# One buffer per chunk for the later quarters' gated values, chunk sums behind the hh sum, and the split of the last pairs in two parts

## The chip, the cores and the metric

The kernel runs on one core of a Trainium2 chip. The metric is the device time of one execution in microseconds (us); lower is better. All times below are in us unless a unit stands beside them. The engines are TensorE (PE in the profile; its weight loads are PEld), VectorE (DVE), ScalarE (ACT), GpSimd (POOL) and SyncE (SP), whose queue issues the DMA transfers.

## The reference

One layer in two halves, on x of 2048 rows and 448 columns, in float32:

```python
h  = x + Re(DFT_seq(DFT_hid(layernorm(x))))
n  = layernorm(h)
h2 = h + (gelu(n @ w_gate) * (n @ w_up)) @ w_down      # 448 -> 1792 -> 448
```

The transforms are products with given cosine and sine matrices. The kernel computes each float32 product from float16 parts: a value is split into a high half (its float16) and a low half (what is left, as float16), and high x high, high x low and low x high are added up.

## The kernel before

**The stages.** Up to about 460 us the kernel does the two Fourier products (lines 481 to 606). What the change touches comes after them: the gate and up products, the gating and the down product, a loop of 42 steps `t`. The 2048 rows are four quarters. Steps 0 to 13 take quarters 0 and 1 together (512 columns at a time), steps 14 to 27 quarter 2, steps 28 to 41 quarter 3 (256 columns). In each of the three passes a step handles one of the 14 blocks of 128 hidden features. From step 14 on a step also does the down product for some chunks. A chunk `d` is one of 8 row pairs `p` times one of `NC` = 7 feature groups `n`: `p, n = divmod(d, 7)`. Pairs 0 to 3 belong to the first pass, 4 and 5 to quarter 2, 6 and 7 to quarter 3. `CHUNK_COUNT` gives each step one or two chunks.

**A step from 14 on** is written out by hand in the main loop (from line 1592), and every engine takes its instructions in the order in which they are written:

- `c_last` and `c_mul` finish the values of the step before: ScalarE applies gelu to its `c`, then `hh = hh * c` (line 1339; GpSimd, in steps 15 to 28 VectorE);
- `x_close`, `z_open`: TensorE's matmuls into banks X and Z (banks of PSUM). There is one bank Z, so `z_open` waits until the last reader of the step before is done with it;
- for the chunks of step t+1, `dn_hi` (ScalarE) and `dn_lo` (VectorE, line 112) make the high and low halves `dn_w`, the weights of the down product;
- for the chunks of step t+2, `dn_sums` makes the sums `dn_s` that this product needs (Strassen's scheme): two on GpSimd (lines 1362, 1363) and one on VectorE (line 1364), the *chunk sum* below;
- `y_mid`: six matmuls into bank Y, then ScalarE's copy `u3` (line 1310) and the *hh sum*: VectorE reads bank Z and writes a value to hh (line 1261);
- the rest of the chunks' down matmuls (line 1191), `x_open` of the next step, `y_close` and `z_close`: more matmuls into Y and Z. `z_close` adds to bank Z and must wait for the hh sum. VectorE then reads Y (line 1327, into hh) and Z (line 1261, into `c`). These two free the banks;
- `y_open` of the next step.

**The values of the gating.** In the first pass the gated values go from `hid` tiles through DRAM (`hid_dram`, line 1323) and come back as chunks `hid_in` (line 1351). In quarters 2 and 3 they stay on the chip, each quarter in one buffer: hh2, from byte 122080 of a partition to 150752, allocated in step 14 over the memory of the first pass's tiles; the four `hid` tiles lay from 142560 to 150752. hh3 is allocated in step 28. The framework puts in the waits between engines. Memory that a tile takes over from an older tile is waited for by the new tile's first writer, tile against tile. A step writes hh at feature group `n`: in quarter 2, steps 14 and 21 write group 0, steps 15 and 22 group 1 and so on; in quarter 3, two steps after each other write one group.

**The last pairs.** Chunks of pairs 6 and 7 are needed after step 41 only. Some are prepared before: `at(side, (t, k), ...)` puts work at place `k` of step `t`; place 6 is behind the hh sum, place 7 the end of the step. Chunk (6, n) has its sums, all on VectorE, at place 6 of step 30 + 2n, and its split, `dn_hi` and `dn_lo` together, at place 7 of the next step. Chunks (7, 0) and (7, 1) follow in steps 31 and 39. There are three `dn_s` buffers; one is free again after its `dn_lo`.

Of the kernel before, what the change touches and what calls it, by code (L numbers as in the profile page):

```python
# [10 lines left out]
F32 = mybir.dt.float32  # L11
# [3 lines left out]
P = 128  # L15
S, D, DF = 2048, 448, 1792
NT = S // P
NF = DF // P
# [15 lines left out]
def kernel(  # L34
# [38 lines left out]
    V, A, G, PE = nc.vector, nc.scalar, nc.gpsimd, nc.tensor  # L73
# [682 lines left out]
    def at(t, n, *what):  # L756
        t.setdefault(n, []).extend(what)
# [60 lines left out]
    for k, (i, i2) in enumerate(tiles_of):  # L818
        n = where["F", i]
        if k > 1:  # L820
            t = None
            if k > 2:
                t = fixed(n - 10, 8, "SP", 0.5, lambda u=i // 2: x_load(u), lag=4.5, kind="xload")
            first_pair = -40.0 if k == 2 else 0.0
            own = "0" if k == 2 else ""
            if (i, i2) in by_scalar:
                t = [add("A", 1.75, T[max(n - 6, 0)], lambda c=c, both=(i, i2): x_moments(c, both), begin=T[max(n - 7, 0)] - 13.0, after=[t], kind="xstat") for c in (i, i2)]
            else:
                t = [add("V", 1.35, T[max(n - 6, 0)] + first_pair, lambda i=i, j=i2: x_stats(i, j), begin=T[max(n - 7, 0)] - 13.0, after=[t], kind="xstat" + own)]
            lite = (i, i2) in by_scalar  # L830
            t = add("A", 0.5 if lite else 0.3, T[max(n - 5, 0)] + first_pair, lambda i=i, j=i2: x_root(i, j), after=t, kind="xroot" + own)
            t = chain("V", RSTD if lite else (0.2, 0.1, 0.1, 0.1), T[max(n - 5, 0)] + first_pair, lambda i=i, j=i2: x_rstd_steps(i, j), [t], kind="xrstd" + own)
            t = add("V", 0.15, T[max(n - 5, 0)] + first_pair, lambda i=i, j=i2: x_bias(i, j), after=[t], kind="xbias" + own)
# [114 lines left out]
    for k, f in enumerate(order):  # L948
# [6 lines left out]
        for m in range(4):  # L955
# [4 lines left out]
            t = high  # L960
# [307 lines left out]
    class GateUp:  # L1268
# [44 lines left out]
        def hidden(self, g):  # L1313
            k, n = divmod(self.f, NC)
            if self.q:
                return hh[self.q][:, n, 2 * k + g, :]
            if (self.t, g) not in hid:
                hid[self.t, g] = hidp.tile([P, 4 * P], F32, tag="hid", bufs=HID_BUFS, name=f"hid{self.t}_{g}")
            return hid[self.t, g]
# [34 lines left out]

    def dn_hid(d):
        p, n = divmod(d, NC)
        return hid_in[d] if p < 4 else hh[p // 2][:, n, :, p % 2 * P : (p % 2 + 1) * P]

    def dn_sums(d, E=G):
        t = dn_hid(d)  # L1360
        s = dn_s[d] = fpool.tile([P, 5, P], F32, tag="dn_s", bufs=DN_S, name=f"dn_s{d}")
        E.tensor_add(s[:, 0:2], t[:, 0:2], t[:, 2:4])
        E.tensor_sub(s[:, 2:4], t[:, 1:4:2], t[:, 0:4:2])
        V.tensor_add(s[:, 4], t[:, 0], t[:, 3])  # L1364

    def dn_split(d, place=None):
        dn_hi(d, place)
        dn_lo(d)
# [4 lines left out]
    def dn_hi(d, place=None):  # L1373
        if place is None:
            place = fpool.tile([P, 2, 7, P], F16, tag="dn_w", bufs=4, name=f"dn_w{d}")
        dn_w[d] = place
        for src, dst in dn_parts(d):
            hi_part(place[:, 0, dst], src)

    def dn_lo(d):  # L1380
        w = dn_w[d]
        for src, dst in dn_parts(d):
            lo_part(w[:, 1, dst], src, w[:, 0, dst])
        dn_s.pop(d)
# [34 lines left out]
    def spare(k, d):  # L1419
        if k < 3:  # L1420
            if "ops" not in spares:
                spares["ops"] = ops3[0][:, 1].rearrange("p o d -> p (o d)")
            t = spares["ops"][:, k * 14 * P : (k + 1) * 14 * P]
            return t.rearrange("p (l a d) -> p l a d", l=2, a=7)
        return fops.tile([P, 2, 7, P], F16, tag=("xn", "tt", "xs")[k - 3], name=f"dn_w{d}")
# [19 lines left out]
    def do(t, k):  # L1445
        for what in side.pop((t, k), ()):
            what()
# [23 lines left out]
    for q in (3,):  # L1471
        for j in range(2):
            t0 = NF + 6 * j
            for f, k, what in (
# [16 lines left out]
            ):  # L1491
                at(side, (t0 + f, k), what)

    for n in range(6):
        t = 2 * NF + 2 * n + 2
        at(side, (t, 6), lambda n=n: dn_sums(6 * NC + n, V))
        at(side, (t + 1, 7), lambda n=n: dn_split(6 * NC + n, spare(n, 6 * NC + n) if n < 4 else None))
    for n, t in enumerate((2 * NF + 3, 2 * NF + 11)):
        at(side, (t, 6), lambda n=n: dn_sums(7 * NC + n, V))
        at(side, (t + 1, 7), lambda n=n: dn_split(7 * NC + n, spare(4 + n, 7 * NC + n)))  # L1500

    drains = {}
    for p in range(6):
# [45 lines left out]
    for t in range(N_GU):  # L1549
        q, f = STEPS[t]  # L1550
        ahead = {0: (), 11: (14,), 12: (), 13: (15,), 14: (16,)}.get(t, (t + 3,) if t < NF else (t + 2,))
        for s in ahead:
            if s < N_GU and s not in LATE:
                gw_load(s)
        if t in (N_GU - 2, N_GU - 1):
            hr_load(t - N_GU + 8)
        nxt = GateUp(t + 1) if t + 1 < N_GU else None
        if q == 0:
            do(t, 0)
            cur.x_close()  # L1560
            nxt.x_open()
            if prev:
                prev.c_last()
                prev.c_mul()
                prev.store(0)
            cur.y_mid()
            late_prep(2 * t)
            do(t, 1)
            down_prep(2 * t)
            if prev:  # L1570
                prev.store(1)
            nxt.z_open()
            nxt.y_open()
            cur.y_close()
            cur.z_close()
            if t >= 10:
                for d in chunks({10: NF, 11: NF + 1, 13: NF + 2}.get(t)):
                    hid_load(d)
            for d in chunks(t + 2):
                done.add(d)  # L1580
                dn_hi(d)
                dn_lo(d)
            if t < NF - 1:
                for d in chunks(t + 3):
                    dn_sums(d)
            do(t, 2)
            down_prep(2 * t + 1)
            late_prep(2 * t + 1)
            do(t, 4)
        else:  # L1590
            mms = [(d, k) for d in chunks(t) for k in range(21)]

            def some(a, b):
                n = len(chunks(t))
                for d, k in mms[a * n : b * n]:
                    dn_mm(d, range(k, k + 1))

            do(t, 0)
            prev.c_last()
            if t == NF:  # L1600
                prev.c_mul()
                for g in range(2):
                    prev.store(g)
                half0.close()
                later = ctx.enter_context(tc.tile_pool(name="later", bufs=1, side="right", reuse_waits="tile"))
                hh[2] = later.tile([P, NC, 4, TQ], F32, name="hh2")
                ops3.append(ring.tile([P, 2, N_OPS, 2 * P], F16, tag="ops", bufs=1, name="ops3"))
                hops[3] = ops3[0][:, 0]
            elif t > 2 * NF:
                prev.c_mul()  # L1610
            for d in chunks(t + 3):
                if d < 4 * NC and t + 3 < 2 * NF + 2 and d not in hid_in:
                    hid_load(d)
            cur.x_close()
            if t > NF:
                cur.z_open()
            nexts = [d for d in chunks(t + 1) if d not in done]
            if t == 2 * NF - 1:
                nexts += [d for d in chunks(t + 2) if d < 4 * NC]
            done.update(nexts)  # L1620
            sums = [d for d in chunks(t + 2) if d not in dn_w and d not in dn_s]
            if t == 2 * NF - 2:
                sums += [d for d in chunks(t + 3) if d < 4 * NC]
            for d in nexts[:1]:
                if d not in dn_w:
                    dn_hi(d)
                dn_lo(d)
            for d in sums[:1]:
                dn_sums(d)
            for d in nexts[1:]:  # L1630
                dn_hi(d)
                dn_lo(d)
            for d in sums[1:]:
                dn_sums(d)
            some(0, 8)
            if t == 2 * NF:
                quarter2.close()
                last = ctx.enter_context(tc.tile_pool(name="last", bufs=1, reuse_waits="tile"))
                hh[3] = last.tile([P, NC, 4, TQ], F32, name="hh3")
            cur.y_mid()  # L1640
            if NF < t <= 2 * NF:
                prev.c_mul(V)
            do(t, 6)
            some(8, 18)
            if nxt:
                nxt.x_open()
            do(t, 1)
            if not nxt:
                some(18, 21)
            do(t, 4)  # L1650
            cur.y_close()
            cur.z_close()
            if nxt:
                some(18, 21)
            do(t, 5)
            for d in chunks(t + 2)[:1]:
                if d not in dn_w and t < N_GU - 1:
                    dn_hi(d)
            if nxt:
                nxt.y_open()  # L1660
            do(t, 2)
            do(t, 3)
            do(t, 7)
        prev, cur = cur, nxt
# [108 lines left out]
```

## Time and profile before

| | us |
|---|---|
| time, median of 3 runs (lowest to highest) | 718.28 (717.92 to 718.44) |
| the profiled execution: its own time | 719.02 |
| its span, from the first to the last instruction | 717.2 |
| PE busy in the span | 695.8 (97%) |
| DVE busy | 589.4 (82%) |
| ACT busy | 415.7 (58%) |
| POOL busy | 172.6 (24%) |

The profile is that of one execution. In a timeline a line is: start and length in us, engine, source line, operation, what it writes and reads (buffer numbers left out), how many; in square brackets how long the engine stood idle before it and what ended that. In the chain of work that ended last a line is: start, length, engine, tile, source line, count. SPq is SyncE's queue issuing a transfer. Steps 14 to 27 take about 8 us each with two chunks and 6 with one; step 14 begins at about 468 us, step 28 at about 588, and the last matmul ends at about 714.

### The profile page before, as it was taken

To read this page: it belongs to the slowest core of one execution; us is meant where nothing else is said; L and a number is where in the kernel's file an instruction comes from. 1 tells how busy PE (TensorE), PEld (TensorE's weight loads), DVE (VectorE), ACT (ScalarE), POOL (GpSimd) and SP (SyncE) were. 2 spreads that over 40 slices of the span, in tenths; PEclk is the share of its full clock that TensorE was granted. 3 is DMA by queue.
4 is the path that set the end of the run, shared out by engine and by line. 5 is a ranking of instruction groups with operands and counts; after the bars stand their busy time and mean duration, and the time that the engine had idled before them with its cause. 6 is when DMAs were issued, how large, how long until landed. Compare 5 with 4: busy or idle time off the path is not lost.

```text
span 717.2 us, 14542 instructions
## 1 busy us (share of the span) xinstructions
PE 695.8 (97%) x5644; PEld 545.4 (76%) x5644; DVE 589.4 (82%) x1112; ACT 415.7 (58%) x800; POOL 172.6 (24%) x198
## 2 busy tenths in 40 slices
PE   8999999999999999999999999959999999989998
PEld 5455779888888888888644444449999989889898
DVE  6999999999998998899477968744878876787776
ACT  5789754766675766466458666524545534555442
POOL 0000000000000000000133534533556464555442
PEclk9999999999999999999999999989999999999999
DMA  9535336567697787776567697974685763535301
GB/s 340 140 97 111 109 128 211 204 203 210 198 233 210 218 220 210 237 247 232 202 195 274 210 304 252 267 210 161 224 206 221 263 164 129 178 132 178 132 27 53
DMA packets 95381, 138.77 MB, mean 193 GB/s; under 512 B 42192, under 2 KB 71120, under 8 KB 95312
## 3 DMA queue, kind: packets, MB, share of 16 engines
q1 hardware_dynamic: 95312, 137.85, 62.2%
q8 instruction: 44, 0.72, 0.4%
q14 instruction: 25, 0.20, 0.1%
HBM read 100.99 MB, written 27.53 MB: 179 GB/s over the span
## 4 chain that ended last, share of the span: by engine, by line
PE 75%; DVE 14%; DMA 6%; issue 3%; ACT 2%; SPq 1%; DVEq 0%; ACTq 0%
PE acc L605 26%; PE acc_d L1191 13%; PE pY L1251 12%; PE pZ L1251 9%; PE pX L1251 8%; PE ab L484 7%; DMA wr<-in_w_seq_dram 3%; DVE dn_w L112 2%; DVE wss L114 1%; DVE ws L114 1%; DMA hid_dram<-hid 1%; DVE dn_s L1364 1%; DMA hid_in<-hid_dram 1%; DVE wsum L549 1%; DMA xT<-xs 1%
## 5 line engine op out<-in xcount | busy, mean ns | idle before, releaser
L1251 PEld LDWEIGHTS <-gw 128*128 128x128 f16 x1638 | 160.6, 98 | 91.2 <-issue 15.4
L605 PE MATMUL acc<-b,ws 128*128 128x224 f16 (+1 forms) x1248 | 187.1, 288 | 0.0
L605 PEld LDWEIGHTS <-ws 128*128 128x128 f16 x1248 | 120.8, 98 | 35.6 <-DVE ws L114 0.2
L605 PE MATMUL acc<-b,wss 128*128 128x224 f16 x1152 | 142.2, 259 | 2.0 <-DVE wss L114 1.9
L1191 PE MATMUL acc_d<-wd,dn_w 128*128 128x224 f16 x1050 | 116.1, 260 | 0.0
L605 PEld LDWEIGHTS <-wss 128*128 128x128 f16 x1152 | 110.8, 98 | 2.7 <-DVE wss L114 2.7
L1191 PEld LDWEIGHTS <-dn_w 128*128 128x128 f16 x1050 | 101.3, 98 | 2.2
L249 POOL TENSOR_TENSOR wd_s<-wd 128x448 f32<-128x448 f32 x7 | 8.8, 1264 | 378.5 <-DMA wd<-in_w_down_dram 350.2
L1251 PE MATMUL pY<-hops,gw 128*128 128x512 f16 (+1 forms) x476 | 89.4, 328 | 0.0
L108 ACT ACTIVATE wss<-wsum 128x1024 f16<-128x1024 f32 x48 | 50.7, 1055 | 48.8 <-DVE wsum L553 28.7
L108 ACT ACTIVATE ws<-wr 128x768 f16<-128x768 f32 (+1 forms) x64 | 56.3, 887 | 27.9 <-DMA wr<-in_w_seq_dram 13.9
L484 PE MATMUL ab<-wh,xT 128*128 128x448 f16 x352 | 69.1, 352 | 1.8 <-ACT xT L446 0.5
L1251 PE MATMUL pZ<-hops,gw 128*128 128x512 f16 (+1 forms) x308 | 59.9, 328 | 9.3 <-DVE hh L1261 8.4
L114 DVE SCALAR_TENSOR_TENSOR ws<-wr,ws 128x768 f16<-128x768 f32 (+1 forms) x64 | 64.8, 1017 | 0.0
L114 DVE SCALAR_TENSOR_TENSOR wss<-wsum,wss 128x1024 f16<-128x1024 f32 x48 | 58.5, 1219 | 7.0 <-ACT wss L108 6.7
L484 PEld LDWEIGHTS <-xT 128*128 128x128 f16 x352 | 33.9, 98 | 33.9 <-issue 1.8
L1251 PE MATMUL pX<-hops,gw 128*128 128x512 f16 (+1 forms) x308 | 57.2, 327 | 0.0
L112 DVE TENSOR_TENSOR dn_w<-dn_s,dn_w 128x640 f16<-128x640 f32 x50 | 51.9, 1039 | 2.4 <-ACT dn_w L108 2.3
L1182 POOL TENSOR_TENSOR hr<-hr,v 128x224 f32<-128x224 f32 x56 | 44.3, 815 | 12.3 <-ACT v L1150 11.9
L1291 ACT ACTIVATE pY<-pX 128x256 f32<-128x256 f32 (+1 forms) x42 | 18.5, 441 | 48.2 <-PE pX L1251 48.2
L1296 ACT ACTIVATE u<-pY 128x256 f32<-128x256 f32 (+1 forms) x42 | 19.0, 453 | 40.5 <-PE pY L1251 40.5
L108 ACT ACTIVATE dn_w<-dn_s 128x640 f16<-128x640 f32 x50 | 36.5, 730 | 7.0 <-DVE dn_s L1364 6.9
(141 smaller groups left out, 991.2 us busy)
## 6 DMA issues: line engine op xcount, KB each, us to landing
wr<-in_w_seq_dram SPq DMA_DIRECT2D x64, 512.0 KB, 4.2
gw<-w_dram SPq DMA_DIRECT2D x36, 896.0 KB, 4.9
gu_raw<-in_w_gu_dram SPq DMA_DIRECT2D x28, 384.0 KB, 4.4
hid_dram<-hid SPq DMA_DIRECT2D x28, 256.0 KB, 5.0
hid_in<-hid_dram SPq DMA_DIRECT2D x28, 256.0 KB, 5.1
w_dram<-gu_p SPq DMA_DIRECT2D x24, 256.0 KB, 2.6
w_dram<-gw SPq DMA_DIRECT2D x6, 896.0 KB, 5.6
hx<-in_x_dram SPq DMA_DIRECT2D x8, 448.0 KB, 4.6
```

What stands on the lines that cost most here:

```text
L108: A.activation(dst, src, AF.Copy, scale=scale)
L112: V.tensor_sub(dst, src, hi)
L114: V.scalar_tensor_tensor(dst, src, scale, hi, op0=ALU.mult, op1=ALU.subtract)
L249: G.tensor_sub(s[:, 2:4], t[:, 0:2], t[:, 2:4])
L484: PE.matmul(feat[i][r][:, :D], xT[i][:, kx, :], w[:, kw, r * D : (r + 1) * D], start=n == 0, stop=n == 10,)
L549: V.tensor_add(s[:, 0:2], r[:, 0:1].to_broadcast([P, 2, 2 * P]), r[:, 1:3])
L605: PE.matmul(banks[k][:, cols], lhs, rhs, start=k not in begun, stop=stop, skip_group_check=True)
L1182: op(x, x, m)
L1191: PE.matmul(acc[k // 2][:, k % 2 * HD : (k % 2 + 1) * HD], a_of(la, a), b_of(lb, b), start=first and m == 0 and k % 2 == 0, stop=last and ...
L1251: PE.matmul(ps, w[:, wl, wa + ws, :], ops[:, m + ms, :], start=first and n == 0, stop=last and n == len(terms) - 1, skip_group_check=True,)
L1291: A.activation(self.Y, self.X, AF.Copy)
L1296: A.activation(self.u2, self.Y, AF.Copy, scale=SC)
```

## The change

Three edits. First, `hh[2]` and `hh[3]` become lists of seven tiles of 4096 bytes a partition, one per feature group: hh2_0 from byte 122080, hh2_5 from 142560, hh2_6 from 146656. Second, the chunk sums of a step go behind the hh sum and `c_mul`. Third, for the early chunks of pairs 6 and 7 the split is taken apart: the high halves stay at place 7 of step t+1, the low halves move to place 6 of step t+2, behind the hh sum there.

```diff
         def hidden(self, g):
...
-                return hh[self.q][:, n, 2 * k + g, :]
+                return hh[self.q][n][:, 2 * k + g, :]
...
-        return hid_in[d] if p < 4 else hh[p // 2][:, n, :, p % 2 * P : (p % 2 + 1) * P]
+        return hid_in[d] if p < 4 else hh[p // 2][n][:, :, p % 2 * P : (p % 2 + 1) * P]
...
+    def ahead_of(d, t, place):
+        at(side, (t, 6), lambda: dn_sums(d, V))
+        at(side, (t + 1, 7), lambda: dn_hi(d, place()))
+        at(side, (t + 2, 6) if t + 2 < N_GU else (t + 1, 7), lambda: dn_lo(d))
+
     for n in range(6):
-        t = 2 * NF + 2 * n + 2
-        at(side, (t, 6), lambda n=n: dn_sums(6 * NC + n, V))
-        at(side, (t + 1, 7), lambda n=n: dn_split(6 * NC + n, spare(n, 6 * NC + n) if n < 4 else None))
-    for n, t in enumerate((2 * NF + 3, 2 * NF + 11)):
-        at(side, (t, 6), lambda n=n: dn_sums(7 * NC + n, V))
-        at(side, (t + 1, 7), lambda n=n: dn_split(7 * NC + n, spare(4 + n, 7 * NC + n)))
+        ahead_of(6 * NC + n, 2 * NF + 2 * n + 2, lambda n=n: spare(n, 6 * NC + n) if n < 4 else None)
+        if n in (0, 4):
+            k = n // 4
+            ahead_of(7 * NC + k, 2 * NF + 2 * n + 3, lambda k=k: spare(4 + k, 7 * NC + k))
...
-                hh[2] = later.tile([P, NC, 4, TQ], F32, name="hh2")
+                hh[2] = [later.tile([P, 4, TQ], F32, name=f"hh2_{n}") for n in range(NC)]
...
-            for d in sums[:1]:
-                dn_sums(d)
             for d in nexts[1:]:
                 dn_hi(d)
                 dn_lo(d)
-            for d in sums[1:]:
-                dn_sums(d)
             some(0, 8)
...
-                hh[3] = last.tile([P, NC, 4, TQ], F32, name="hh3")
+                hh[3] = [last.tile([P, 4, TQ], F32, name=f"hh3_{n}") for n in range(NC)]
             cur.y_mid()
             if NF < t <= 2 * NF:
                 prev.c_mul(V)
+            for d in sums:
+                dn_sums(d)
             do(t, 6)
```

VectorE in step 14, before. The first two rows are the chunk sums of chunks 4 and 5, `hh_5801` is hh2, `pZ` and `pY` are the banks; DMAHW names are transfers that a row waits for:

```order
L112 TENSOR_TENSOR dn_w_5785<-dn_s_5708,dn_w_5785 128x640 [waits Activation_49]
L1364 TENSOR_TENSOR dn_s_5812<-hid_in_5776 128x128 [waits DMAHW3_49]
L1364 TENSOR_TENSOR dn_s_5816<-hid_in_5778 128x128 [waits DMAHW4_49,DVE_49]
L1261 SCALAR_TENSOR_TENSOR hh_5801<-pZ_5747,u_14_5846 128x256 [waits DMAHW2_49,DMAHW6_49,DMAHW1_49,DMAHW7_49,Activation_49,Pool_49]
L173 SCALAR_TENSOR_TENSOR nb_h_0_5878<-mv_h_0_4370,r_h_0_4417 128x2
L1327 SCALAR_TENSOR_TENSOR hh_5801<-pY_5731,g_14_5810 128x256 [waits PE_49]
L1261 SCALAR_TENSOR_TENSOR c_14_5894<-pZ_5747,u_14_5760 128x256 [waits PE_49]
```

And now (`hh_0_5801` is the tile of group 0):

```order
L112 TENSOR_TENSOR dn_w_5785<-dn_s_5708,dn_w_5785 128x640 [waits Activation_49]
L1261 SCALAR_TENSOR_TENSOR hh_0_5801<-pZ_5747,u_14_5844 128x256 [waits Activation_49]
L1364 TENSOR_TENSOR dn_s_5847<-hid_in_5776 128x128 [waits DMAHW3_49]
L1364 TENSOR_TENSOR dn_s_5851<-hid_in_5778 128x128 [waits DMAHW4_49,DVE_49]
L173 SCALAR_TENSOR_TENSOR nb_h_0_5884<-mv_h_0_4370,r_h_0_4417 128x2
L1327 SCALAR_TENSOR_TENSOR hh_0_5801<-pY_5731,g_14_5816 128x256 [waits PE_49]
L1261 SCALAR_TENSOR_TENSOR c_14_5900<-pZ_5747,u_14_5760 128x256 [waits PE_49,Pool_49]
```

The hh sum stands ahead of the two chunk sums, and of its waits only that for ScalarE is left. The four transfers that it waited for were the stores of the last `hid` tiles; that for hh2_6 now stands at its first writer, in step 20.

VectorE in step 34, before, from the end of step 33. `ops` is where the halves of chunk (6, 1) go, `hh_7539` is hh3, and `hh_5801` hh2; `dn_s_8167` holds the sums of chunk (6, 2):

```order
L112 TENSOR_TENSOR ops_5802<-hh_7539,ops_5802 128x256 [waits Activation_49]
L112 TENSOR_TENSOR ops_5802<-dn_s_7971,ops_5802 128x640 [waits Activation_49]
L112 TENSOR_TENSOR dn_w_8104<-hh_5801,dn_w_8104 128x256
L112 TENSOR_TENSOR dn_w_8104<-dn_s_8048,dn_w_8104 128x640 [waits DVE_49,Pool_49]
L1364 TENSOR_TENSOR dn_s_8142<-hh_5801 128x128
L1364 TENSOR_TENSOR dn_s_8146<-hh_5801 128x128 [waits DVE_49]
L1261 SCALAR_TENSOR_TENSOR hh_7539<-pZ_8133,u_34_8164 128x256 [waits Activation_49]
L1362 TENSOR_TENSOR dn_s_8167<-hh_7539 128x256 [waits DVE_49,Pool_49]
L1363 TENSOR_TENSOR dn_s_8167<-hh_7539 128x256
L1364 TENSOR_TENSOR dn_s_8167<-hh_7539 128x128
L1327 SCALAR_TENSOR_TENSOR hh_7539<-pY_8086,g_34_8131 128x256 [waits PE_49]
L1261 SCALAR_TENSOR_TENSOR c_34_8201<-pZ_8133,u_34_8113 128x256 [waits PE_49]
```

And now:

```order
L112 TENSOR_TENSOR dn_w_8116<-hh_6_5807,dn_w_8116 128x256 [waits Activation_49]
L112 TENSOR_TENSOR dn_w_8116<-dn_s_8075,dn_w_8116 128x640 [waits Activation_49]
L1261 SCALAR_TENSOR_TENSOR hh_3_7540<-pZ_8143,u_34_8166 128x256 [waits Activation_49]
L1364 TENSOR_TENSOR dn_s_8169<-hh_0_5801 128x128 [waits DVE_49]
L1364 TENSOR_TENSOR dn_s_8173<-hh_1_5802 128x128 [waits DVE_49]
L112 TENSOR_TENSOR ops_5808<-hh_1_7538,ops_5808 128x256
L112 TENSOR_TENSOR ops_5808<-dn_s_7983,ops_5808 128x640
L1362 TENSOR_TENSOR dn_s_8179<-hh_2_7539 128x256 [waits DVE_49,Pool_49]
L1363 TENSOR_TENSOR dn_s_8179<-hh_2_7539 128x256
L1364 TENSOR_TENSOR dn_s_8179<-hh_2_7539 128x128
L1327 SCALAR_TENSOR_TENSOR hh_3_7540<-pY_8098,g_34_8141 128x256 [waits PE_49]
L1261 SCALAR_TENSOR_TENSOR c_34_8213<-pZ_8143,u_34_8125 128x256 [waits PE_49]
```

The two low halves of chunk (6, 1) and the two chunk sums went from ahead of the hh sum to behind it, and stand between it and the two rows that free the banks. Each other engine keeps its order over the whole program.

## The prediction

> **What bounds the kernel now.** I read the busy table by stretches first, then TensorE's waits, then the timeline around the longest of them, then the chain. The last stage (steps 14 to 41, from 468 us on) is bound by TensorE: from 490 to 560 us it is busy for 69.5 of 70 us. The 20 us before that are the exception (columns: stretch, its length, PE, PEld, DVE, ACT, POOL busy, granted clock, DMA share, GB/s):
>
> ```profile
> 470.00:490.00 20.00, 13.14 (x111) 11.44 (x110) 8.69 (x16) 5.49 (x12) 8.32 (x10) 0.83 0.60 182
> 490.00:560.00 70.00, 69.47 (x677) 65.29 (x675) 52.34 (x108) 35.03 (x87) 34.52 (x45) 1.00 0.67 211
> ```
>
> TensorE's waits from 470 us on have nearly all one form (us in total, times, longest):
>
> ```profile
> PE pZ L1251 <- DVE hh L1261: 11.8, 7, 6.9
> ```
>
> These are the closing matmuls of bank Z, five of them, which wait until VectorE's hh sum (line 1261, called by `y_mid`) has read the bank. The longest stands in step 14, in the timeline:
>
> ```profile
> 470.82 0.39 ACT L1310 ACTIVATE u<-pY 128x256 f32<-128x256 f32 x1 [1.10 <-PE pY L1251]
> 472.01 1.20 SPq L1323 DMA_DIRECT2D hid_dram<-hid  x2
> 473.13 0.71 PE L1251 MATMUL pY<-hops,gw 128*128 128x256 f16 x5
> 474.99 0.29 DVE L1364 TENSOR_TENSOR dn_s<-hid_in 128x128 f32<-128x128 f32 x1 [2.26 <-DMA hid_in<-hid_dram]
> 480.18 0.33 SPq L1351 DMA_DIRECT2D hid_in<-hid_dram  x1
> 480.22 0.42 DVE L1261 SCALAR_TENSOR_TENSOR hh<-pZ,u 128x256 f32<-128x256 f32 x1 [4.93 <-DMA hid_dram<-hid]
> 480.70 1.23 PE L1251 MATMUL pZ<-hops,gw 128*128 128x256 f16 x5 [6.86 <-DVE hh L1261]
> 483.34 1.19 POOL L1362 TENSOR_TENSOR dn_s<-hid_in 128x256 f32<-128x256 f32 x1 [6.79 <-DMA hid_in<-hid_dram]
> ```
>
> The hh sum had its operand `u` at 471.21. It stood first behind a chunk sum that waited for a load (474.99), then for the stores of the old `hid` tiles: the one buffer hh2 lies over their memory. TensorE stood still and then ran slowly, as the chain shows; its later pieces are the same kinds at full speed:
>
> ```profile
> 480.70 1.23 PE pZ L1251 x5
> 481.92 1.12 PE acc_d L1191 x6
> 483.04 1.28 PE pY L1251 x6
> 484.32 0.84 PE pX L1251 x5
> 485.16 0.66 PE pZ L1251 x6
> ...
> 488.00 1.92 PE acc_d L1191 x20
> ...
> 493.44 0.66 PE pZ L1251 x6
> ...
> 515.19 0.57 PE acc_d L1191 x6
> ...
> 516.42 0.55 PE pX L1251 x5
> ```
>
> **Part 1, the wait in step 14.** The order shows that hh_0's first write now waits for ScalarE alone: buffer 0 lies below the `hid` tiles, and only buffers 5 and 6 (steps 19 and 20, 40 us later) lie on them. The two chunk sums now stand behind it. So it can run at 472.0, when the low halves ahead of it are done, and the closing matmuls start when the five before them end: 473.13 + 0.55 = 473.68, not 480.70: 7.02 saved. The four pieces from 480.70 to 485.16 take 4.46; at full speed five, six, six and five matmuls take 0.55 + 0.57 + 0.66 + 0.55 = 2.33: 2.13 more. Together 9.15.
>
> The Trainium skill ("TensorE: Matmul & The Clock Gate", Part 1) says that an idle window of about 3.4 us halves the clock and about 3.4 busy us restore it. By that the slow stretch would cost at most some 1.7 us, an estimate, and the whole gain would be 0.4 smaller; the granted clock of 0.83 agrees in kind.
>
> What is late next? Behind the hh sum now stand the chunk sums and, behind them on VectorE, the sums that free bank Y and bank Z (lines 1327 and 1261 into `c`). Bank Z is opened again by step 15 at 473.68 + 2.33 = 476.0. The second chunk sum ends at 475.3 (its load does not move), two sums of 0.42 follow: 476.2, a wait of 0.2. The next Z opening comes 493.44 - 485.16 = 8.28 later, at 484.5. Before it, step 15's chunk sum waits for a load that can only be issued when the store has landed (480.18) and was there by 483.34: with 0.28 to 0.81 for the sum and twice 0.42, `c` is done between 484.4 and 485.0. I take 0.1. Part 1: 9.15 - 0.3 = **8.85**.
>
> **Part 2, the other waits.** All of TensorE's from 490 us on, in the timeline:
>
> ```profile
> 514.48 0.71 PE L1251 MATMUL pZ<-hops,gw 128*128 128x256 f16 x5 [0.53 <-DVE hh L1261]
> 578.00 0.71 PE L1251 MATMUL pZ<-hops,gw 128*128 128x256 f16 x5 [1.05 <-DVE hh L1261]
> 623.07 0.71 PE L1251 MATMUL pZ<-ops,gw 128*128 128x256 f16 x5 [0.68 <-DVE hh L1261]
> 630.18 0.71 PE L1251 MATMUL pZ<-ops,gw 128*128 128x256 f16 x5 [0.58 <-DVE hh L1261]
> 638.02 0.71 PE L1251 MATMUL pZ<-ops,gw 128*128 128x256 f16 x5 [1.41 <-DVE hh L1261]
> 666.21 0.71 PE L1251 MATMUL pZ<-ops,gw 128*128 128x256 f16 x5 [0.68 <-DVE hh L1261]
> 668.81 0.81 PE L1251 MATMUL pZ<-ops,gw 128*128 128x256 f16 x6 [0.40 <-DVE c L1261]
> ```
>
> Each costs 0.16 more than its bracket, since the piece after it takes 0.71 instead of 0.55. The first two (steps 18 and 26) are the hh sum behind chunk sums, at 578.00 behind one that waited for its load. Moving the chunk sums behind it removes both. The cover they move into is long: with two chunks in a step, Z is opened 493.44 - 488.00 = 5.44 after `y_mid`'s last matmul. By the rows of Part 3 the hh sum starts 0.52 after it and takes 0.42, `c_mul` 0.41 to 0.95 (the low half of that size), two chunk sums 0.56 to 1.54, the two sums behind them 0.84: `c` is done 2.75 to 4.3 after it. **1.9** saved.
>
> **Part 3, steps 32, 34 and 38.** The other five (3.75, with 0.16 each 4.55) go as well: chunk sums and the low halves of the last pairs no longer stand ahead of the hh sum. But in steps 32, 34, 36 and 38 both, and the sums of the next last chunk, now stand between the hh sum and `c`. What that takes, from VectorE's rows:
>
> ```profile
> 488.52 0.42 DVE L1261 SCALAR_TENSOR_TENSOR hh<-pZ,u 128x256 f32<-128x256 f32 x1 [1.09 <-ACT u L1310]
> ...
> 633.96 0.95 DVE L112 TENSOR_TENSOR dn_w<-hh,dn_w 128x256 f16<-128x256 f32 x1
> 634.83 1.34 DVE L112 TENSOR_TENSOR dn_w<-dn_s,dn_w 128x640 f16<-128x640 f32 x1
> 636.09 1.54 DVE L1364 TENSOR_TENSOR dn_s<-hh 128x128 f32<-128x128 f32 x2
> 637.56 0.41 DVE L1261 SCALAR_TENSOR_TENSOR hh<-pZ,u 128x256 f32<-128x256 f32 x1
> ...
> 638.76 0.28 DVE L1364 TENSOR_TENSOR dn_s<-hh 128x128 f32<-128x128 f32 x1
> ...
> 639.30 0.41 DVE L1261 SCALAR_TENSOR_TENSOR c<-pZ,u 128x256 f32<-128x256 f32 x1
> ...
> 654.74 0.41 DVE L112 TENSOR_TENSOR dn_w<-hh,dn_w 128x256 f16<-128x256 f32 x1
> 655.07 0.81 DVE L112 TENSOR_TENSOR dn_w<-dn_s,dn_w 128x640 f16<-128x640 f32 x1
> ```
>
> and from the chain, in step 40, which has one chunk and no wait:
>
> ```profile
> 677.32 0.96 PE acc_d L1191 x10
> ...
> 681.51 0.66 PE pZ L1251 x6
> ```
>
> With one chunk in the step, Z is opened 681.51 - 677.32 = 4.19 after `y_mid`'s last matmul. The hh sum starts 0.52 after it (488.52 against 488.00). From hh sum to the end of `c`, with one last chunk's sums between, step 34 takes 639.71 - 637.56 = 2.15. Added are the low halves, 1.14 alone (654.74 to 655.88) or 2.21 beside GpSimd (633.96 to 636.17), and two chunk sums, 0.56 alone or 1.54. So `c` ends 4.4 to 6.4 after `y_mid`: a wait of 0.2 to 2.2 in step 34. GpSimd's four sums fall in that very time there, so I take 1.6. With one chunk sum (steps 32 and 38; 36 has 5.44 of cover) it ends at 4.1 to 5.65: up to 1.45; GpSimd has fewer sums there and starts them early, so 0.3 each. New waits 2.2, with about 0.15 each 2.65 in all (bounds 0 and 5.9). Part 3: 4.55 - 2.65 = **1.9**, between -1.35 and 4.55.
>
> **What costs nothing.** The orders of TensorE, ScalarE, GpSimd and SyncE stay as they are; only VectorE's changes, and no instruction is added. GpSimd's `dn_s` in steps 34, 37 and 39 newly wait for the later low halves; the idle stretches before its `c_mul` cover that. The tail after step 41 runs its matmuls back to back and keeps its order.
>
> **The sum.** 8.85 + 1.9 + 1.9 = 12.65. The profiled execution took 719.02 (span 717.2 and 1.8 around it) and becomes 706.4; the median of the runs is 718.28, 0.7 below it, and becomes **705.6**.
>
> **The rivals.**
>
> *A. The load takes the place of the store (20%).* Step 15's chunk sum waits on VectorE with `c` behind it; the load landed 3.16 after its issue. The rows of `hid_in` (waits, and time to landing):
>
> ```profile
>   DVE dn_s L1364: 3.9, 2
> ...
> DMA to landing us min/median/max: 3.0/5.1/7.3
> ```
>
> At the median, TensorE loses 1.9 more (707.5), at the slowest 4.1 (709.7). For it: the median. Against it: the same load, in the same queue position, took 3.16.
>
> *B. `c` is late in every even step (18%).* If VectorE's operations always wait for GpSimd's, Part 3 goes to its bound of -1.35: 708.9. For it: 1.34 against 0.81 for the same low half. Against it: the low halves now start when much of GpSimd's work is over. The Trainium skill ("SBUF — State Buffer", "SBUF: two separate sides") has a rule for this: a two-input VectorE operation and a GpSimd operation that reads SBUF share a port pair under an exclusive lock, and the loser waits for the whole instruction. By that rule the far end is the true one.
>
> *C. The wait does not go (3%).* If hh_0 still met the stores, only Parts 2 and 3 remain: 714.5. The order speaks against it.
>
> *D. Slower (3%).* Every chunk sum of steps 15 to 25 could hold up `c` on VectorE behind a late load. It decides from the point where the loads land more than about 4.4 us after `y_mid` (the cover of 5.44 less 1.0 for what follows); to lose the 12.65, eleven steps must each lose over 1.15, and at 1.3 the time would be 718.28 - 12.65 + 14.3 = 719.9. Against it: VectorE waited for such a load only twice, 3.9 in all (the row under A), and the loads are issued a step ahead.
>
> **How the numbers follow.** The forecast has 56%. All waits gone would be 15.6 saved, 702.7; A at the median and B together give 10.8: 9.15 - 0.3 - 1.9 + 1.9 - 1.35 = 7.5 saved, 710.8. The range is 703.2 to 710.8. A measurement of this kernel can tell about 0.2% (1.4 us): faster by more 0.95 (forecast, A, B, most of C), within it 0.02 (C with A, or a D that stops short), slower 0.03 (D and what is like it).
>
> **What would show it.** In the profile after: no wait of pZ near 474 us, the clock of that stretch at 1.0 instead of 0.83, the hh sum ahead of the chunk sums, no wait of pZ for hh above 0.3; a wait of pZ for `c` in step 34 of 1 to 2 us and small ones in steps 32 and 38. Wrong would be: a wait of several us between 474 and 486 (Part 1), or waits for `c` in steps 15 to 27.

## The result, and the profile after

The changed kernel takes 709.43 (median of 4 runs, 708.02 to 710.04), beside 718.36 of the kernel before on the same chip (717.92 to 720.24): a ratio of 0.9868, with a 95% interval of 0.9844 to 0.9892. That is 8.9 saved; 12.65 was forecast. The profiled execution took 708.02, with a span of 706.2. Below, a step's time is the distance from its first six matmuls into bank Z (the row `pZ ... x6`) to those of the next step; undisturbed it is 8.28 with two chunks and 6.27 with one.

The busy table by stretches (columns as in the prediction) and the two rows of TensorE's waits (us in total, times, longest), of the kernel after:

```profile
470.00:490.00 20.00, 19.92 (x196) 18.69 (x194) 12.87 (x27) 8.93 (x22) 7.67 (x10) 1.00 0.75 242
490.00:560.00 70.00, 70.00 (x683) 65.91 (x681) 60.14 (x115) 37.65 (x93) 40.30 (x49) 1.00 0.71 220
560.00:640.00 80.00, 76.66 (x741) 71.50 (x739) 55.29 (x111) 37.84 (x95) 42.02 (x54) 1.00 0.51 162
640.00:690.00 50.00, 47.80 (x471) 45.22 (x469) 35.21 (x72) 21.67 (x52) 21.73 (x27) 1.00 0.29 102
```

```profile
PE pZ L1251 <- DVE c L1261: 4.4, 4, 1.7
PE pZ L1251 <- DVE hh L1261: 1.1, 1, 1.1
```

In the first stretch TensorE is busy for 19.92 of 20 us instead of 13.14, at a clock of 1.00 instead of 0.83. Its waits for the hh sum fell from 11.8 to 1.1, but a kind that the kernel before hardly had, the wait for `c`, now takes 4.4, and all of it stands behind 560. The timeline of the first stretch:

```profile
471.02 0.41 DVE L1261 SCALAR_TENSOR_TENSOR hh<-pZ,u 128x256 f32<-128x256 f32 x1
472.24 0.71 PE L1251 MATMUL pZ<-hops,gw 128*128 128x256 f16 x5
472.47 0.29 DVE L1364 TENSOR_TENSOR dn_s<-hid_in 128x128 f32<-128x128 f32 x1 [0.64 <-DMA hid_in<-hid_dram]
474.56 0.82 PE L1251 MATMUL pZ<-hops,gw 128*128 128x256 f16 x6
478.65 0.33 SPq L1351 DMA_DIRECT2D hid_in<-hid_dram  x1
482.08 0.29 DVE L1364 TENSOR_TENSOR dn_s<-hid_in 128x128 f32<-128x128 f32 x1 [3.04 <-DMA hid_in<-hid_dram]
482.62 0.41 DVE L1261 SCALAR_TENSOR_TENSOR c<-pZ,u 128x256 f32<-128x256 f32 x1
483.09 0.82 PE L1251 MATMUL pZ<-hops,gw 128*128 128x256 f16 x6
```

The closing matmuls at 472.24 have no wait, and the hh sum stands ahead of the chunk sum that waits for its load. The opening at 483.09, that of step 16, is 0.25 late (483.09 - 474.56 = 8.53 instead of 8.28), because `c` stands behind the chunk sum of 482.08.

The stages of all profiled executions, cut at the Z openings of steps 14, 16, 29 and 41; step 14 opens at 463.46 before and at 462.04 after, while step 13 is still under way. The 1.4 between those two lie ahead of every touched instruction, and from step 41's opening on both take 35.9, so the touched part gives 217.88 - 208.29 = 9.6. The expectations below call the last two columns steps 16 to 28 and 29 to 41.

| kernel | steps 14, 15 | steps 16 to 28 | steps 29 to 40 |
|---|---|---|---|
| before | 29.82 | 103.89 | 84.17 |
| after | 21.05 | 102.89 | 84.35 |
| forecast for after | 20.97 | 101.99 | 82.27 |
| after, a second time (e11) | 21.62 | 102.85 | 84.36 |
| e1 buffers alone | 25.10 | 105.01 | 84.17 |
| e2 chunk sums alone | 30.06 | 104.08 | 83.13 |
| e3 low halves alone | 28.79 | 103.52 | 82.98 |
| e4 buffers and chunk sums | 22.62 | 103.23 | 83.13 |
| e5 after, drains in odd steps | 21.24 | 103.12 | 82.23 |
| e7 after, load of chunk 27 earlier | 20.98 | 101.97 | 84.35 |
| e8 after, last pairs' sums in odd steps | 21.03 | 103.31 | 80.26 |
| e9 e7 and e8 together | 22.97 | 102.04 | 80.25 |
| e10 e9, and sums behind `c` in 14, 15 | 20.80 | 101.97 | 80.27 |

The forecast row is that of before less 8.85, 1.9 and 1.9.

### The profile page after: what moved, and what is told of

The parts are those of the page before. It is cut to its first block, busy times and chain, and to the rows that moved or that the text cites. A ratio compares the mean times of both kernels' runs of the same rounds, so it can differ in the third digit from the quotient of the medians.

```text
span 706.2 us, 14542 instructions
## 1 busy us (share of the span) xinstructions
PE 692.6 (98%) x5644; PEld 544.7 (77%) x5644; DVE 586.6 (83%) x1112; ACT 416.1 (59%) x800; POOL 169.6 (24%) x198
## 4 chain that ended last, share of the span: by engine, by line
PE 80%; DVE 11%; DMA 5%; issue 1%; ACT 1%; SPq 1%; ACTq 0%; DVEq 0%
PE acc L605 29%; PE acc_d L1191 14%; PE pY L1251 13%; PE pZ L1251 9%; PE pX L1251 8%; PE ab L484 7%; DMA wr<-in_w_seq_dram 2%; DVE ws L114 1%; DMA hid_dram<-hid 1%; DVE dn_w L112 1%; DVE wss L114 1%; DVE wsum L549 1%; DVE ops L112 1%; DVE dn_s L1364 1%; DMA x<-in_x_dram 1%
## 5 line engine op out<-in xcount | busy, mean ns | idle before, releaser
L112 DVE TENSOR_TENSOR dn_w<-dn_s,dn_w 128x640 f16<-128x640 f32 x50 | 49.9, 998 | 1.8 <-ACT dn_w L108 1.5
L1261 DVE SCALAR_TENSOR_TENSOR hh<-pZ,u 128x256 f32<-128x256 f32 x28 | 11.8, 420 | 34.4 <-ACT u L1310 34.3
```

The lines of the kernel that those rows point to most:

```text
L112: V.tensor_sub(dst, src, hi)
L1261: V.scalar_tensor_tensor(dst, ps, SC, other, op0=ALU.mult, op1=ALU.add)
```

## The experiments

**Which edit carries Part 1.** Three kernels with one edit each, and one with the first two; all were timed beside the same runs of before (717.79).

*e1*, the first edit alone:

```diff
...
-                hh[2] = later.tile([P, NC, 4, TQ], F32, name="hh2")
+                hh[2] = [later.tile([P, 4, TQ], F32, name=f"hh2_{n}") for n in range(NC)]
...
-                hh[3] = last.tile([P, NC, 4, TQ], F32, name="hh3")
+                hh[3] = [last.tile([P, 4, TQ], F32, name=f"hh3_{n}") for n in range(NC)]
```

> Only the buffers per chunk; the order of before. Theory (the wait of step 14 is two waits, for the stores and for a load, and the buffers take the first): the hh sum of step 14 runs when the chunk sum ahead of it has its load, about 475.3 on before's clock, so the closing matmuls of bank Z wait about 2 us instead of 6.9 and the clock stays full: 7 us faster than before, 711; the waits of steps 18, 26 and 32 to 38 stay as in before. Rival (the order of the sums carries the step-14 gain): the wait stays above 5 us and the time above 716.

Measured: 714.95, ratio 0.9956 (0.9936 to 0.9976). The stores are no longer waited for, but half the gain is lost one step later, as e1's timeline and its busy table show:

```profile
481.43 0.29 DVE L1364 TENSOR_TENSOR dn_s<-hid_in 128x128 f32<-128x128 f32 x1 [5.51 <-DMA hid_in<-hid_dram]
484.23 0.71 PE L1251 MATMUL pZ<-hops,gw 128*128 128x256 f16 x5 [3.32 <-DVE hh L1261]
486.55 0.82 PE L1251 MATMUL pZ<-hops,gw 128*128 128x256 f16 x6
```

```profile
470.00:490.00 20.00, 16.02 (x156) 14.81 (x154) 11.30 (x22) 7.73 (x18) 7.28 (x10) 1.00 0.71 229
```

The chunk sum waits 5.51 for its load, with the hh sum still behind it, and TensorE waits 3.32 in step 15. The load takes the store's place, and the expectation, which had no load in step 15, missed by 4.

*e2*, the second edit alone:

```diff
-            for d in sums[:1]:
-                dn_sums(d)
...
-            for d in sums[1:]:
-                dn_sums(d)
...
             cur.y_mid()
...
+            for d in sums:
+                dn_sums(d)
```

> Only the chunk sums behind the hh sum; one buffer, low halves where they were. Theory: the hh sum of step 14 still waits for the stores, to about 480, so nothing is gained there; the waits of steps 18, 26 and 32 to 38 for the hh sum go (4 us), little new waiting for c: about 714. Rival (the chunk sums, not the low halves, make the new waits for c in steps 32 to 38): 4 us of waits for c appear and the time is 718.

Measured: 715.93, ratio 0.9973 (0.9957 to 0.9990). Step 14 keeps its wait in e2's timeline, since the hh sum still meets the stores:

```profile
479.32 1.23 PE L1251 MATMUL pZ<-hops,gw 128*128 128x256 f16 x5 [7.57 <-DVE hh L1261]
```

Of the 1.9 by which its median is lower, the profile shows 1.04, in steps 29 to 40; the other two stages are 0.2 longer each. The waits for the hh sum go from steps 18, 26 and 32 to 38, as expected, but waits for `c` of 0.34, 0.67, 1.01 and 1.13 come up in steps 26, 32, 34 and 38, most of what the rival had named, and step 27 now waits 1.79 for its hh sum.

*e3*, the third edit alone:

```diff
-        at(side, (t + 1, 7), lambda n=n: dn_split(6 * NC + n, spare(n, 6 * NC + n) if n < 4 else None))
...
+        at(side, (t + 1, 7), lambda: dn_hi(d, place()))
+        at(side, (t + 2, 6) if t + 2 < N_GU else (t + 1, 7), lambda: dn_lo(d))
```

> Only the low halves of the last pairs one step later; one buffer, chunk sums ahead of the hh sum. Theory (the low halves between the hh sum and c make the waits for c): waits for c of 2 to 3 us in all in steps 32 to 38 in place of 3.8 for the hh sum, so about 717, and the wait of 6.9 in step 14 stays. Rival (the low halves' move is what helps the later steps): no waits for c and no waits for the hh sum there, 714.

Measured: 716.97, ratio 0.9984 (0.9963 to 1.0006): no change that a time could show. The profile shows 1.19 less in steps 29 to 40, with waits for `c` of 0.54, 0.69, 0.34 and 1.47 in steps 32, 34, 36 and 38: 3.0 in all, as its theory had it.

*e4*, the changed kernel with the third edit undone:

```diff
...
-        at(side, (t + 1, 7), lambda: dn_hi(d, place()))
-        at(side, (t + 2, 6) if t + 2 < N_GU else (t + 1, 7), lambda: dn_lo(d))
...
+        at(side, (t + 1, 7), lambda n=n: dn_split(6 * NC + n, spare(n, 6 * NC + n) if n < 4 else None))
...
```

> The whole change but for the low halves, which stay with the high halves at the end of the step before. Theory: no wait in step 14, none for the hh sum in 32 to 38 and none above 0.3 for c: 4 us faster than the whole change, about 705. Rival (the chunk sums make the waits for c): the waits of 4.4 us for c stay and the time is the whole change's, 709.

Measured: 707.67, ratio 0.9854 (0.9827 to 0.9881), not to be told from the changed kernel (0.9868). So Part 1 needs both edits: 4.72 with the buffers alone, nothing with the order alone, 6.9 to 8.8 with both (e9 the least). But e4's theory failed in the later steps: without the low halves, the waits for `c` of e2 stand there again, in steps 32, 34 and 38.

```profile
616.21 0.82 PE L1251 MATMUL pZ<-ops,gw 128*128 128x256 f16 x6 [0.67 <-DVE c L1261]
630.02 0.82 PE L1251 MATMUL pZ<-ops,gw 128*128 128x256 f16 x6 [1.01 <-DVE c L1261]
658.77 0.82 PE L1251 MATMUL pZ<-ops,gw 128*128 128x256 f16 x6 [1.13 <-DVE c L1261]
```

And the third edit brings nothing on top. In steps 29 to 40 chunk sums alone save 1.04, low halves alone 1.19, both together lose 0.18; against e4 the third edit costs 1.22 there (84.35 instead of 83.13). Each takes work from ahead of the hh sum, and both put it in one place, between hh sum and `c`.

**The new waits for `c`.** The timeline of step 38 after: VectorE, and GpSimd's *drain* (line 1182, four operations), the additions that finish a pair's output rows before they are stored:

```profile
652.44 0.42 DVE L1261 SCALAR_TENSOR_TENSOR hh<-pZ,u 128x256 f32<-128x256 f32 x1 [2.48 <-ACT u L1310]
652.78 0.50 DVE L1364 TENSOR_TENSOR dn_s<-hh 128x128 f32<-128x128 f32 x1
653.09 3.50 POOL L1182 TENSOR_TENSOR hr<-hr,v 128x224 f32<-128x224 f32 x4
653.21 0.87 DVE L112 TENSOR_TENSOR dn_w<-hh,dn_w 128x256 f16<-128x256 f32 x1
654.00 1.28 DVE L112 TENSOR_TENSOR dn_w<-dn_s,dn_w 128x640 f16<-128x640 f32 x1
655.20 0.87 DVE L1362 TENSOR_TENSOR dn_s<-hh 128x256 f32<-128x256 f32 x1
656.00 0.87 DVE L1363 TENSOR_TENSOR dn_s<-hh 128x256 f32<-128x256 f32 x1
657.33 0.41 DVE L1261 SCALAR_TENSOR_TENSOR c<-pZ,u 128x256 f32<-128x256 f32 x1
657.79 0.82 PE L1251 MATMUL pZ<-ops,gw 128*128 128x256 f16 x6 [1.67 <-DVE c L1261]
```

The hh sum starts on time, and everything behind it is stretched. Two theories: GpSimd's drains do it, or VectorE's work is too long in any case. *e5* moves the drains of pair 4 by a step:

```diff
-            after = 1 + n if p != 4 else 1 + n // 2 * 2
+            after = 1 + n if p != 4 else 2 + n // 2 * 2
```

> The changed kernel with one thing moved: GpSimd's drain of pair 4's output rows (line 1182, four operations at a time) goes from the ends of steps 36 and 38 ahead of its place to steps 37 and 39, in which VectorE has no low halves of the last pairs between the hh sum and c. Theory (the new waits of steps 36 and 38 come from these drains: they stretch VectorE's low halves from 0.41 and 0.81 to 0.87 and 1.28 and its chunk sums from 0.42 to 0.87): the waits for c of steps 36 (0.54) and 38 (1.67) go, about 2.5 with what follows them, and the time is about 707 against 709.4 of the changed kernel; steps 29 to 41 take 82.0 instead of 84.35. Rival (VectorE simply has too much to do between hh sum and c, whatever GpSimd does): the waits stay within 0.3 of what they are, 709.4, 84.3.

Measured: 706.20, ratio 0.9836 (0.9791 to 0.9880), an interval that overlaps with that of the change; the profile decides. The same step in e5's timeline:

```profile
651.43 0.42 DVE L1261 SCALAR_TENSOR_TENSOR hh<-pZ,u 128x256 f32<-128x256 f32 x1 [2.48 <-ACT u L1310]
652.19 0.41 DVE L112 TENSOR_TENSOR dn_w<-hh,dn_w 128x256 f16<-128x256 f32 x1
652.52 0.81 DVE L112 TENSOR_TENSOR dn_w<-dn_s,dn_w 128x640 f16<-128x640 f32 x1
653.26 0.41 DVE L1362 TENSOR_TENSOR dn_s<-hh 128x256 f32<-128x256 f32 x1
653.60 0.41 DVE L1363 TENSOR_TENSOR dn_s<-hh 128x256 f32<-128x256 f32 x1
654.47 0.41 DVE L1261 SCALAR_TENSOR_TENSOR c<-pZ,u 128x256 f32<-128x256 f32 x1
654.95 0.82 PE L1251 MATMUL pZ<-ops,gw 128*128 128x256 f16 x6
```

The same instructions, from hh sum to `c`: 654.47 - 651.43 = 3.04 instead of 657.33 - 652.44 = 4.89, and no wait. Steps 36 and 38 take 8.28 and 6.27, undisturbed; the stage takes 2.1 less, with 0.43 come up in step 39, where the drain now stands. In these two steps it was the drains.

*e8* leaves the drains and takes work away: the sums of chunks (6, 1) to (6, 4) go to the odd steps.

```diff
-        at(side, (t, 6), lambda: dn_sums(d, V))
+        at(side, (t + (6 * NC < d < 6 * NC + 5), 6), lambda: dn_sums(d, V))
```

> The changed kernel with the sums of the early chunks (6, 1) to (6, 4) moved one step later, from the even steps 32 to 38, where the low halves stand, to the odd steps 33 to 39 (still behind the hh sum). Then no step but 39 and 40 has both. Theory (VectorE's work between hh sum and c is what is too long, and a step's room is about 3.7 with one chunk of the down product): each even step loses 1.1 to 2.1 of that work, the waits for c of steps 32, 34, 36 and 38 (0.95, 1.29, 0.54, 1.67) fall to 0.3 or less each, and at most 0.5 comes up in step 39: about 4 saved, 705.5 against 709.4; steps 29 to 41 take 80.5 to 81.5 instead of 84.35. Rival (the low halves alone hold up c, or the odd steps, in which one chunk's work and GpSimd's own sums are, get the same waits): less than 1.5 saved, 708 or more.

Measured: 705.12, ratio 0.9807 (0.9772 to 0.9842). How much longer than undisturbed the steps are, in us:

| step | 32 | 33 | 34 | 36 | 38 | 39 | sum |
|---|---|---|---|---|---|---|---|
| before | 0.94 | 0.74 | 1.58 | 0.26 | 1.41 | 0 | 4.93 |
| after | 1.12 | 0 | 1.45 | 0.70 | 1.83 | 0 | 5.10 |
| e3, low halves alone | 0.71 | 0 | 0.85 | 0.50 | 1.63 | 0 | 3.69 |
| e4, no low halves moved | 0.94 | 0 | 1.27 | 0.26 | 1.40 | 0 | 3.87 |
| e5 | 1.11 | 0 | 1.45 | 0 | 0 | 0.43 | 2.99 |
| e8 | 0.05 | 0.87 | 0.05 | 0 | 0.04 | 0 | 1.01 |

The four waits go. Step 34, which has no drain, keeps 1.45 in e5 and loses it in e8, so less work is enough there. That isn't the amount alone: in the profile of after its two chunk sums take 1.24 where two alone take 0.56, and a low half 0.94 instead of 0.41, beside GpSimd's own sums. No run moved those sums alone. In steps 36 and 38 either cure is enough. What comes up instead is 0.87 in step 33, where the low halves of chunk (7, 0) and the moved sums of (6, 1) meet beside a drain; the expectation had looked for it in step 39.

**The wait that came back in step 27.** From the timeline of after: SyncE's queue, VectorE and TensorE in steps 26 and 27:

```profile
558.09 0.39 SPq L1415 DMA_DIRECT2D out_dram<-hr  x1
...
559.08 0.56 SPq L1351 DMA_DIRECT2D hid_in<-hid_dram  x1
...
566.46 0.29 DVE L1364 TENSOR_TENSOR dn_s<-hid_in 128x128 f32<-128x128 f32 x1 [1.39 <-DMA hid_in<-hid_dram]
...
569.51 1.28 DVE L112 TENSOR_TENSOR dn_w<-dn_s,dn_w 128x640 f16<-128x640 f32 x1
...
574.91 0.41 DVE L1261 SCALAR_TENSOR_TENSOR hh<-pZ,u 128x256 f32<-128x256 f32 x1
...
575.38 0.71 PE L1251 MATMUL pZ<-hops,gw 128*128 128x256 f16 x5 [1.10 <-DVE hh L1261]
```

Chunk 27's load is issued behind a store of output rows and lands some 7 us later. From then on VectorE works without a pause, three chunks' low halves among it, up to the hh sum that TensorE waits for. *e7* puts the load ahead of the store:

```diff
+    at(side, (2 * NF - 3, 2), lambda: hid_load(4 * NC - 1))
```

> The changed kernel with the load of chunk 27 ahead of the store of pair 1's output rows in SyncE's queue instead of behind it. Theory (in the changed kernel this load is issued at 559.08, after a store that waits for GpSimd's drain, lands at 566.4, and so the chunk sum, c and three chunks' low halves come late on VectorE and TensorE waits 1.10 for the hh sum of step 27): the load lands before the hh sum of step 26 is done, that wait of 1.10 goes, 1.2 saved with what follows: about 708.2 against 709.4, steps 16 to 28 take 101.7 instead of 102.9. Rival (VectorE is full in steps 26 and 27, with six operations on low halves beside GpSimd's, and the load only sets the end by chance): the wait shrinks by less than 0.5, 709.0 or more.

Measured: 708.96, ratio 0.9867 (0.9829 to 0.9905). The time can't tell it from the changed kernel; e7's profile can:

```profile
555.31 0.53 SPq L1351 DMA_DIRECT2D hid_in<-hid_dram  x1
...
564.74 2.21 DVE L1364 TENSOR_TENSOR dn_s<-hid_in 128x128 f32<-128x128 f32 x3
...
574.08 0.71 PE L1251 MATMUL pZ<-hops,gw 128*128 128x256 f16 x5 [0.18 <-DVE hh L1261]
```

The wait falls to 0.18 and the stage by 0.92. So the load set the end there. The room was short for a second reason: in the profile of after all six low halves of step 27 were stretched beside GpSimd (0.88 to 0.94 and 1.28 to 1.35 instead of 0.41 and 0.81), by 3.0 in all. No run takes that away alone.

**Both cures, and the loads of steps 14 and 15.** *e9* has the edits of e7 and e8 together.

> Both of the last two edits on the changed kernel: the load of chunk 27 ahead of the store, and the sums of chunks (6, 1) to (6, 4) in the odd steps. If the waits are independent, as they lie in different steps, the savings add: 1.2 and 4, about 704.3 against 709.4 of the changed kernel. If the saved time of one comes back as a wait of the other, about 705.5.

Measured: 703.80, ratio 0.9786 (0.9753 to 0.9819). In the stages the savings add (102.04 and 80.25), but this execution lost 2.17 in steps 14 and 15, where `c` stood behind chunk sums that waited for their loads. *e10* adds this:

```diff
-            for d in sums:
+            for d in sums if t > NF + 1 else ():
                 dn_sums(d)
...
             cur.z_close()
+            for d in sums if t <= NF + 1 else ():
+                dn_sums(d)
```

> The kernel of the experiment before this one (sums of (6, 1) to (6, 4) in odd steps, load of chunk 27 ahead of the store), and in steps 14 and 15 alone the chunk sums behind the sum into c, no longer between the hh sum and c. Theory (what is left in steps 14 and 15, and what spreads these steps between 20.98 and 22.97 from one profile to another, is the load of the chunk sum, with c behind it on VectorE): the two steps take 20.8 or less whatever the loads do, no wait for c there, and the time is 0.5 to 2 lower: about 702.5, against 703.8. Rival (the load is needed early anyway: the halves of these chunks, which feed step 16's down matmuls, and the hh sum of the next step behind them, come late instead): the same wait stands a little later, as a wait for the hh sum of step 15 or 16; 21 to 23 for the two steps or for the three with step 16, 703.8.

Measured: 703.64, ratio 0.9817 (0.9780 to 0.9855); the before beside it took 718.01, that beside e9 719.59. The first stretch of e10's profile has no gap left, and the two steps take 20.80, undisturbed:

```profile
470.00:490.00 20.00, 20.00 (x197) 18.85 (x195) 13.67 (x28) 9.58 (x23) 8.51 (x12) 1.00 0.76 246
```

The median is only 0.16 below e9's, and against its own before it saved less, 14.4 instead of 15.8: of its four runs two took 702.08, as forecast, the others 705.20 and 706.99, and those have no profile. Whether the edit is worth anything stays open. e8 and e9 beat both the kernel before and the changed kernel: their intervals lie below that of the change (0.9844 to 0.9892); e10's reaches into it.

*e11* is the changed kernel again.

> The changed kernel unchanged, beside the others on one chip, to see how far its stages move from one execution to another. If the reading of the first profile holds, steps 29 to 41 take 84.35 again, with the waits for c of 0.95, 1.29, 0.54 and 1.67, within 0.1 (they hang on no transfer), steps 16 to 28 take 102.9 to 103.3, and steps 14 and 15, which hang on loads, 21 to 23; the time is 708 to 711. If those waits were of that one execution, some of them are missing or another stands for them.

Measured: 708.17, ratio 0.9874 (0.9846 to 0.9901). The waits for `c` in steps 32, 34, 36 and 38 are 0.95, 1.29, 0.54 and 1.68, as in the first profile: they hang on no transfer. Steps 14 and 15 differ by 0.57.

## Why the prediction was right, and where it was not

The median came out 3.8 above the forecast. In the profiles the touched part gained 9.6 instead of 12.65; the 3.05 that are missing are 0.1 in Part 1, 0.9 in Part 2 and 2.1 in Part 3. Outside that part, the steps ahead of it gave 1.4 that nobody had forecast, and the profiled execution, which the forecast put 0.8 above the median, was the fastest of four, 1.4 below it. The lower end of the range, 703.2, isn't worked out from the parts; with all waits gone they give 702.7.

**Part 1 was right, at its fair-weather end.** It gained 8.77, forecast 8.85. The undisturbed two steps (20.80 in e10) are 9.02 below before, against 9.15: 7.04 of wait, forecast 7.02, and 1.98 of slow clock (from the closing matmuls to the next opening 485.00 - 480.70 = 4.30 before, 474.56 - 472.24 = 2.32 after), forecast 2.13. The opening in before:

```profile
485.00 0.82 PE L1251 MATMUL pZ<-hops,gw 128*128 128x256 f16 x6
```

What is left of the loads varies, though. Taking 20.80 off, the seven executions with both edits (after, e4, e5, e7, e8, e9, e11) lost 0.25, 1.82, 0.44, 0.18, 0.23, 2.17 and 0.82, 0.84 in the mean where I took 0.3. Most of it, 0 to 1.83, stands in step 14, behind the load of its second chunk sum, which I had put at 0.2 from one landing. Rival A's load, in step 15, cost 0.25, 0.59 and 0.78 in three of the seven (after, e11, e9) and nothing in the others; in e11 and e9 it shows as waits for `c` of 0.43 and 0.61, which the prediction had named as a sign of being wrong. Rival A is no other world but the same kernel on other executions. The side of before varies too (29.82, 30.06 in e2, 28.79 in e3), and the means of the two sides are 7.9 apart. So the mechanism is shown, but the agreement within 0.1 is luck.

**Part 2 was mis-sized.** Both waits went (0.69 in step 18, 1.22 in step 26). Step 27 went from 0.29 to 1.26 above undisturbed, so 1.0 was kept of 1.9, and its wait of 1.10 for the hh sum is against the sign "no wait of pZ for hh above 0.3". I had checked the cover ahead of `c` for that step, not the cover ahead of the *next* hh sum: VectorE's rows from the late load to step 27's hh sum are one unbroken run. Moving TensorE's wait away let it arrive there earlier, while the load set VectorE's time. e7 shows it. The size varies as well: e1, which keeps the old order, lost 1.05 in step 18 and 1.85 in step 26, where before lost 0.69 and 1.22.

**Part 3 is the step that failed.** "New waits 2.2, with about 0.15 each 2.65 in all" came to 5.10, so that the part lost 0.18 instead of gaining 1.9. For step 34 the price held: 1.6 plus 0.15 forecast, 1.45 measured. Wrong was the sentence that gave steps 32 and 38 0.3 each because "GpSimd has fewer sums there", and step 36 nothing because of its longer cover: they took 1.12, 1.83 and 0.70. I had counted GpSimd's chunk sums, not its drains, which run in just these steps; e5 shows that for 36 and 38. In step 32 the drain of pair 3 is there too (2 operations), and two low halves beside it took 0.88 and 1.28 instead of 0.41 and 0.81, 0.94 more of the 1.12; it wasn't moved alone.

Even the far end was too low for 36 and 38. The term "from hh sum to the end of `c`" (2.15) came from step 34 of before, where GpSimd's sums were about over when the last chunk's own sums ran:

```profile
637.89 0.61 DVE L1362 TENSOR_TENSOR dn_s<-hh 128x256 f32<-128x256 f32 x1
638.43 0.41 DVE L1363 TENSOR_TENSOR dn_s<-hh 128x256 f32<-128x256 f32 x1
```

Beside the drain of step 38 the same two took 0.87 each. So the waits there, 1.67 and 0.54, passed the far ends of 1.45 and 0.2, and that the sum of 5.10 stayed under 5.9 is luck: step 34 came out below its own 2.2. In kind it is rival B, for the even steps, by way of the drains.

The rule that stood beside rival B, of the Trainium skill ("SBUF — State Buffer", "SBUF: two separate sides"), says that the loser of the shared port pair waits for the whole instruction. The trace agrees that the two contend; the cost was about 0.46 for each VectorE operation beside the drains (0.41 to 0.87, 0.81 to 1.28), less than the 0.66 that an operation of the drain takes alone.

**What was to cost nothing** cost nothing: the tail after step 41's opening takes 35.9 in both, and GpSimd's product in step 38 still waits for ScalarE's `c`, not for its own sums.

## What to carry to other kernels

Before moving work behind a critical instruction, add up what then stands between it and the *next* thing that the bound engine waits for, at the durations that these operations have beside everything the neighbouring engine does there, its drains and copies too. Two edits that each empty a crowded place can fill the same other place: test them apart and together. When a wait disappears, look one step on for a transfer whose time did not move.

## What the runs showed of the hardware

**What meeting GpSimd costs a VectorE operation depends on GpSimd's operation, not on its own size.** From e4's timeline, four VectorE operations beside a drain:

```profile
641.67 2.97 POOL L1182 TENSOR_TENSOR hr<-hr,v 128x224 f32<-128x224 f32 x4
...
642.58 0.88 DVE L1363 TENSOR_TENSOR dn_s<-hh 128x256 f32<-128x256 f32 x1
643.38 0.74 DVE L1364 TENSOR_TENSOR dn_s<-hh 128x128 f32<-128x128 f32 x1
644.04 0.41 DVE L1327 SCALAR_TENSOR_TENSOR hh<-pY,g 128x256 f32<-128x256 f32 x1
```

With both inputs in SBUF the addition beside these operations of 224 columns is mostly 0.46, whatever VectorE's size: 0.28 to 0.74, 0.41 to 0.88, 0.81 to 1.28. Beside GpSimd's operations of 256 columns it is mostly 0.53 (0.28 to 0.81, 0.81 to 1.34), and beside its products of 512 columns 1.08 (0.41 to 1.49), as in before:

```profile
469.53 1.46 POOL L1339 TENSOR_TENSOR hid<-hid,c 128x512 f32<-128x512 f32 x1 [3.58 <-ACT c L1335]
469.77 1.49 DVE L112 TENSOR_TENSOR dn_w<-hid_in,dn_w 128x256 f16<-128x256 f32 x1
```

Not every operation beside GpSimd pays in full; some get less, some nothing. The sums that read one input from PSUM (`pY` above, `pZ`) stay at 0.41 to 0.43 beside GpSimd in every profile.

**The clock's loss doesn't grow with the wait.** From the end of a wait to the next Z opening, the same 22 matmuls took 2.32 after a wait of 3.32 (e1, clock 1.00), 4.27 after one of 5.87 (e3), 4.30 after one of 6.86 (before) and 3.84 after one of 7.57 (e2, from 479.32 to 483.16). The wait of 3.32 cost its own length alone; the longer ones 1.5 to 2.0 more. The rule of the Trainium skill that stood beside Part 1 ("TensorE: Matmul & The Clock Gate", Part 1: an idle window of about 3.4 us) fits both sides of that; the estimate of at most 1.7 that was worked out from it was passed by two of the three losses (1.95 and 1.98).
